# Attention and gated layer: stores of converted weights and of gated values, issued behind the next step

## The chip, the cores and the metric

The kernel runs on one core of a Trainium2 chip. The time is device microseconds (us) of one execution; the median of several runs counts. Five engines work side by side, each through its own queue and in order: PE (TensorE, matrix products), DVE (VectorE), ACT (ScalarE), POOL (GpSimd) and SP (SyncE, which issues most DMAs here). An instruction whose inputs are missing holds up all that stand behind it on its engine.

## The reference

Attention by random features over 8 batches, 8 heads, 576 positions of 64 values, then a gated layer over the 4608 tokens of 512 values:

```python
def phi(x):                                  # q and k, scaled before
    proj = np.einsum('bhsd,md->bhsm', x, omega)
    h = proj - np.sum(x * x, axis=-1, keepdims=True) / 2.0
    return np.exp(h - np.max(h, axis=-1, keepdims=True)) / np.sqrt(m)
...
kv = np.einsum('bhsm,bhsd->bhmd', k_p, v)
num = np.einsum('bhsm,bhmd->bhsd', q_p, kv)
...
x = np.ascontiguousarray(attn_out.transpose(0, 2, 1, 3)).reshape(B * S, H * D)
gate = 1.0 / (1.0 + np.exp(-(x @ w_gate)))
return (gate * (x @ w_val)) @ w_out          # 512 -> 1536 -> 512
```

The weights `w_gate`, `w_val` and `w_out` arrive as float64 and are converted on the chip.

## The kernel before

The program is written as Python generators. The order in which they record instructions is the program order; a scheduler then orders each engine's queue, by priorities and its own estimate of what is ready, and hands out tile buffers. An instruction passed through `pin` (`tc.keep_in_program_order`) may not stand ahead of the instruction that was recorded last before it on its engine; all others are free to move.

Stages, with their places in the profiled execution:

1. **Attention** (to about 510 us, `attention`, `norms`, `keys`, `queries`): for each of 4 batch pairs, two halves and 4 head pairs. A query step runs PE (projection `ppq`), DVE (`mxq`, `hmq`, `subq`, `hq`), PE (`ptq`), ACT (`qpq`), PE (`pnq`), DVE (`denq`, `invq`, `xq`), PE (`pxq`), ACT (`xsq`), and a DMA of ACT's queue to `xT` in DRAM. SP loads `rawk`, `rawq`, `natk`, `natq`, `v`.
2. **First pass** (`first_pass`, laced into the attention and running to about 590 us): columns 0 to 511 of the hidden layer for 10 chunks of tokens, named by their first token (0, 256, 512, 1024, ... 4096). A chunk's `xT` is loaded into `xr` (one buffer), ACT and POOL split it into four tiles `xe..._0` to `xe..._3` of a high and a low part, and for j = 0 to 3 PE makes two products `gv` of 12 matmuls, the gate (`gv..._j_0`, read by ACT into `ge`) and the value (`gv..._j_1`, read by DVE into `ye`, line 275). `ye` has two buffers and is stored to DRAM on SP (line 280). Until the attention is recorded to its end, the products have two PSUM banks.
3. **Conversion** (`convert_weights`): 14 tiles c0 to c13. Each is loaded on SP in two halves of 512 KB (line 144), each half takes six DVE operations (lines 78 to 94) and one of POOL (line 96), and the tile then four subtractions on POOL (`L180`); it is stored to `w32` in DRAM, 1 MB (line 181). There are two buffers `cv`. The generator `later` is advanced one step for each step of the first pass.
4. **Second pass** (from about 600 us, `second_pass`, `gated`), which needs `u0` to `u7`, loaded from `w32` and split (lines 199, 200, 214, 215); then the output product (`last`). The buffers of `u` and most of those that come late lie where the attention's buffers were, those of `cv` included, so `u0` is loaded only when they are free.

SP's queue is thus shared by the attention's loads, the first pass's loads and stores, and the conversion's loads and stores.

Of the kernel before, what the change touches and what calls it, by code (L numbers as in the profile page):

```python
# [34 lines left out]
NC = 512  # L35
Q = NC // 2
# [3 lines left out]
NE = 4  # L40
EP = NE // 2
WE = 2 * KC * P
# [25 lines left out]
def split(nc, hi, lo, x, lo_engine=None):  # L68

    nc.scalar.activation(out=hi, in_=x, func=AF.Copy)  # L70
    (lo_engine or nc.vector).tensor_tensor(out=lo, in0=x, in1=hi.bitcast(F32), op=ALU.subtract)  # L71


def from_float64(nc, t, a, bits):


    lo, hi = bits[:, :, 0], bits[:, :, 1]
    nc.vector.tensor_scalar(out=a, in0=hi, scalar1=0x7FFFFFFF, scalar2=None, op0=ALU.bitwise_and)

    f = a.bitcast(F32)  # L80
    nc.vector.tensor_scalar(
        out=f, in0=f, scalar1=LARGEST, scalar2=LEAST, op0=ALU.min, op1=ALU.max
    )

    nc.vector.tensor_scalar(
        out=t, in0=a, scalar1=3, scalar2=0x3FFFFFFF, op0=ALU.logical_shift_left, op1=ALU.bitwise_and
    )
    nc.vector.scalar_tensor_tensor(
        out=t, in0=hi, scalar=0xC0000000, in1=t, op0=ALU.bitwise_and, op1=ALU.bitwise_or
    )  # L90

    nc.vector.tensor_scalar(out=a, in0=t, scalar1=0xFF800000, scalar2=None, op0=ALU.bitwise_and)
    r = a.bitcast(F32)
    nc.vector.scalar_tensor_tensor(out=r, in0=lo, scalar=2.0**-52, in1=r, op0=ALU.mult, op1=ALU.mult)
    x = t.bitcast(F32)
    nc.gpsimd.tensor_tensor(out=x, in0=x, in1=r, op=ALU.add)
# [3 lines left out]
def attn_glu_kernel(ctx: ExitStack, tc, qT, kT, qn, kn, va, om, ident, w, out):  # L100
    nc = tc.nc
# [5 lines left out]
    w32 = dram.tile([N_LATE, P, 8, Q], F32, name="w32")  # L107


    ye = dram.tile([EP, P, NCH, 2, 2, 2, P], F32, name="ye")  # L110
# [16 lines left out]
    def any_bank(name):  # L127

        if not cycle:
            return bank("at", name)  # L130
        cycle.append(cycle.pop(0))
        return bank(cycle[-1], name)
# [3 lines left out]
    pin = tc.keep_in_program_order  # L136

    def converted(cv, i):


        raw = [cv[:, (1 + h) * 2 * WP : (2 + h) * 2 * WP] for h in range(2)]
        for h in range(2):
            o = i + h * WP
            nc.sync.dma_start(out=raw[h].rearrange("p (n two) -> p n two", two=2), in_=w[:, o : o + WP, :])
        yield
        for h in range(2):
            from_float64(
                nc, cv[:, h * WP : (h + 1) * WP], cv[:, 6 * WP :],
                raw[h].rearrange("p (n two) -> p n two", two=2),
            )  # L150
            yield
# [13 lines left out]

    def convert_weights(tiles, ns):

        for n in ns:
            cv = tiles(f"c{n}")
            for _ in converted(cv, NE * WE + n * 4 * Q):  # L170
                yield
            f = cv[:, : 4 * WP].bitcast(F32).rearrange("p (b q) -> p b q", q=Q)
            b, t = f[:, :4], f[:, 4:]
            for o, x, y in (
                (t[:, 0], b[:, 3], b[:, 0]),
                (t[:, 2], b[:, 2], b[:, 3]),
                (t[:, 1], b[:, 2], t[:, 0]),
                (t[:, 3], b[:, 1], t[:, 1]),
            ):
                nc.gpsimd.tensor_tensor(out=o, in0=x, in1=y, op=ALU.subtract)  # L180
            nc.sync.dma_start(out=w32[n], in_=f)


    turn = [0]
# [1 line left out]
    def buffer(name, dtype=F32R, at=None):  # L186
        if at is None:
            at = late if turn[0] % (XK + XL) < XL else keep
            turn[0] += 1
        return at.tile([P, 2, NC], dtype, tag="x", bufs=XK if at is keep else XL, name=name)  # L190
# [27 lines left out]
    def load(o, n):  # L218

        raw = keep.tile([P, KC, NC], F32, tag="xr", bufs=1, name=f"xr{o}_{turn[0]}")[:, :, :n]  # L220
        while not ready(o + n):
            next(steps, None)
        for k in range(KC):
            nc.sync.dma_start(out=raw[:, k], in_=xT[k, :, o : o + n])
        return raw

    def first_pass():


        def parts_of(o, n, at):  # L230
            raw = load(o, n)
            yield
            for k in range(KC):
                x = buffer(f"xe{o}_{k}", at=at)[:, :, :n]
                split(nc, x[:, 0], x[:, 1], raw[:, k], lo_engine=nc.gpsimd)
                yield x

        def product(i, j, o, n, x):
            name = f"gv{o}_{j}_{i}"
            gv = (any_bank(name) if late else bank("gv", name))[:, :n]  # L240
            wh, wl = ws[j]
            m = 0
            for k in range(KC):
                s = slice((i * KC + k) * P, (i * KC + k + 1) * P)
                xh, xl = x[k][:, 0], x[k][:, 1]
                for u, v in ((wl, xh), (wh, xl), (wh, xh)):
                    nc.tensor.matmul(gv, lhsT=u[:, s], rhs=v, start=(m == 0), stop=(m == 3 * KC - 1))  # L247
                    m += 1
            return gv


        chunks = [(0, Q), (Q, Q)] + [(c * NC, NC) for c in range(1, NCH)]
        x = [t for t in parts_of(*chunks[0], keep) if t is not None]
        at, homes = keep, []
        for (o, n), after in zip(chunks, chunks[1:] + [None]):
            ahead, parts = [], None
            for j in range(NE):
                if after and parts is None and (j == NE - 1 or late):

                    if late:  # L260
                        homes.append(keep if len(homes) % 2 == 0 else late)
                        at = homes[-1]
                    parts = parts_of(*after, at)
                    next(parts)
                gate = product(0, j, o, n, x)
                g = keep.tile([P, 2, 2, P], F32, tag="g", bufs=2, name=f"ge{o}_{j}")
                flat = g.rearrange("p i s t -> p (i s t)")[:, :n]
                nc.scalar.activation(out=flat, in_=gate, func=AF.Tanh, scale=0.5)
                yield
                if parts and at is late:  # L270
                    ahead += [t for t in (next(parts, None),) if t]
                val = product(1, j, o, n, x)
                y = keep.tile([P, 2, 2, P], F32, tag="y", bufs=2, name=f"ye{o}_{j}")

                nc.vector.scalar_tensor_tensor(
                    out=y.rearrange("p i s t -> p (i s t)")[:, :n], in0=flat, scalar=1.0, in1=val,
                    op0=ALU.add, op1=ALU.mult,
                )
                i = o % NC // Q
                nc.sync.dma_start(out=ye[j // 2, :, o // NC, j % 2, i : i + n // Q], in_=y[:, : n // Q])  # L280
                yield
            x = ahead + list(parts or ())

    def operands(c):

# [108 lines left out]
    def second_pass(x, parts):  # L394


        held = iter(())

        def put():
            while stores:  # L400
                to, y = stores.pop(0)
                pin(nc.sync.dma_start(out=to, in_=y))

        for c in range(NCH):
            ahead = None
            for pair in range(EP, NPAIR):
                g = keep.tile([P, 4, 2, P], F32, tag="g", bufs=2, name=f"gl{pair}_{c}")
                y = keep.tile([P, 2, N_OPS, P], F32, tag="y", bufs=2, name=f"yl{pair}_{c}")
                for kind in range(2):
                    group = gated(c, x, pair, kind, g, y)  # L410
                    next(group)
                    next(held, None)
                    next(group)
                    held = group
                    if pair == EP and kind:
                        assert next(parts, parts) is parts
                        if c < NCH - 1:
                            parts = operands(c + 1)
                            ahead = next(parts)
                    else:  # L420
                        next(parts, None)
                    yield c, pair, kind
                    if kind:
                        put()
            x = ahead
        next(held, None)
        yield NCH, EP, 0
        put()

    def gated_values(c, s, j, raw=None):  # L430
# [279 lines left out]
    stores = []  # L710
    with tc.tile_pool(name="early", bufs=1) as early:
        gates = first_pass()
        with tc.tile_pool(name="a", bufs=1, side="right") as pool:
            steps = attention(pool)

            def tiles(name):
                return pool.tile([P, 7 * WP], U32, tag="cv", bufs=2, name=name)
# [3 lines left out]
            n = 0  # L721
# [7 lines left out]
            n = credit = 0  # L729
# [136 lines left out]
```

## Time and profile before

| | |
|---|---|
| runs | 1236.67, 1238.58, 1239.37 us; median 1238.58 |
| the profiled execution | 1239.43 us, span 1237.6 us |
| mean granted clock of PE | 0.968 |
| chain that ended last | PE 71%, DVE 12%, issue 7%, DMA 5%, POOL 3% |
| DMA | 219.43 MB, 177 GB/s on average |

Times inside the execution are counted from the start of its span. The view of the busy time in stretches gives, for each engine, the busy us of that stretch, and behind them PE's granted clock, the busy share of the DMA engines and GB/s. In the view in order of time the first two numbers of a row are the start and the length, and a bracket at its end is the idle time before it with what ended it. `SPq` rows are DMA issues. A granted clock below 1.00 is the mean share of full speed that PE was given in the stretch.

### The profile page before, as it was taken

Reading aid. Unit: us, or ns where it says so; the run is one execution under the profiler, and the core shown is the slowest. Engines: PE = TensorE matmul, PEld = TensorE weight load, DVE = VectorE, ACT = ScalarE, POOL = GpSimd, SP = SyncE. Lnnn points to the kernel's source line nnn. Section 1 sums busy time; section 2 is a strip of 40 time slices with the busy share of each in tenths; the row PEclk is TensorE's granted clock in tenths of the full one; section 3 lists DMA queues with packets and bytes.
Section 4 is the critical chain, followed back from the end, with each engine's and each line's share of the span. In section 5 each row is a group of like instructions: output and inputs, shape, how many; then the busy total and the mean of one; then the engine's idle time right before and its main releaser. Section 6 shows DMA issues by size and latency. Waiting matters only on the chain.

```text
span 1237.6 us, 23990 instructions
## 1 busy us (share of the span) xinstructions
PE 1172.3 (95%) x8828; PEld 1109.8 (90%) x8828; DVE 864.5 (70%) x1907; ACT 530.7 (43%) x1164; POOL 542.7 (44%) x599
## 2 busy tenths in 40 slices
PE   6798989999898999899899999999998899999998
PEld 5788978798887888788899999999998899999998
DVE  4889888999698866433566656666569777777773
ACT  5556755565455463342423322232325344343331
POOL 2454365556457552131466666666666211111110
PEclk7798989999899999899899999999999999999999
DMA  7667767786657641461432333323337676666662
GB/s 247 213 199 228 210 219 253 238 268 237 226 182 252 223 153 39 139 202 52 152 128 106 123 135 124 121 93 125 124 135 267 203 226 195 188 191 189 198 191 94
DMA packets 104950, 219.43 MB, mean 177 GB/s; under 512 B 11136, under 2 KB 42112, under 8 KB 103040
## 3 DMA queue, kind: packets, MB, share of 16 engines
q1 hardware_dynamic: 87984, 198.94, 48.5%
q10 hardware_dynamic: 16848, 18.95, 4.4%
q8 instruction: 70, 1.15, 0.4%
q14 instruction: 48, 0.39, 0.1%
HBM read 141.82 MB, written 76.02 MB: 176 GB/s over the span
## 4 chain that ended last, share of the span: by engine, by line
PE 71%; DVE 12%; issue 7%; DMA 5%; POOL 3%; ACT 1%; SPq 1%; ACTq 0%; DVEq 0%; POOLq 0%
PE gw L351 27%; PE po L465 20%; PE gv L247 10%; PE pkv L595 4%; PE pnq L638 4%; PE ptq L626 2%; DVE mxq L552 2%; DVE hq L615 1%; DMA xr<-xT 1%; DMA xT<-xsq 1%; DMA rawk<-kT 1%; POOL loq L71 1%; DVE hmq L556 1%; PE ppk L547 1%; POOL xe L71 1%
## 5 line engine op out<-in xcount | busy, mean ns | idle before, releaser
L351 PE MATMUL gw<-xl,u 128*128 128x256 f32 x3024 | 364.6, 283 | 6.9 <-ACT p L362 3.6
L351 PEld LDWEIGHTS gw<-xl,u 128*128 128x128 f32 x3024 | 363.5, 191 | 7.9 <-DVE u L331 3.9
L465 PE MATMUL po<-u,yh 128*128 128x256 f32 x1512 | 272.4, 283 | 0.0
L465 PEld LDWEIGHTS po<-u,yh 128*128 128x128 f32 x1512 | 234.8, 191 | 0.0
L465 PE MATMUL po<-u,yl 128*128 128x256 f32 x756 | 214.0, 283 | 3.3 <-DVE yl L71 3.3
L247 PE MATMUL gv<-xe,wh 128*128 128x512 f32 (+1 forms) x640 | 201.0, 388 | 2.1 <-POOL xe L71 2.1
L70 ACT ACTIVATE yh<-yr 128x896 fp32r<-128x896 f32 x108 | 100.2, 950 | 156.8 <-PE po L465 86.3
L465 PEld LDWEIGHTS po<-u,yl 128*128 128x128 f32 x756 | 144.3, 191 | 3.9 <-DVE yl L71 3.9
L247 PEld LDWEIGHTS gv<-xe,wh 128*128 128x128 f32 x640 | 117.3, 194 | 20.1 <-POOL xe L71 4.5
L71 POOL TENSOR_TENSOR yl<-yr,yh 128x896 fp32r<-128x896 f32 x17 | 38.0, 2232 | 215.3 <-PE po L465 139.9
L247 PE MATMUL gv<-xe,wl 128*128 128x512 f32 (+1 forms) x320 | 125.8, 394 | 2.7 <-POOL wl L71 1.6
L71 DVE TENSOR_TENSOR yl<-yr,yh 128x896 fp32r<-128x896 f32 x91 | 103.0, 1144 | 31.5 <-PE po L465 19.1
L331 DVE TENSOR_TENSOR u<-gw,p 128x256 f32<-128x256 f32 x144 | 60.7, 422 | 59.2 <-PE gw L351 51.1
L595 PE MATMUL pkv<-v,kpk 128*128 128x66 f32 x512 | 84.4, 290 | 13.3 <-ACT kpk L587 12.6
L595 PEld LDWEIGHTS pkv<-v,kpk 128*128 128x128 f32 x512 | 77.0, 209 | 21.5 <-ACT kpk L587 19.8
L71 POOL TENSOR_TENSOR lok<-rawk,hik 128x256 fp32r<-128x256 f32 (+1 forms) x80 | 55.5, 712 | 68.0 <-ACT hik L70 67.6
L456 DVE TENSOR_TENSOR yr<-yr 128x128 f32<-128x128 f32 x144 | 60.1, 451 | 35.3 <-DMA yr<-ye 34.8
L71 POOL TENSOR_TENSOR xe<-xr,xe 128x512 fp32r<-128x512 f32 (+1 forms) x40 | 49.1, 1244 | 74.2 <-ACT xe L70 62.4
L71 POOL TENSOR_TENSOR loq<-rawq,hiq 128x256 fp32r<-128x256 f32 (+1 forms) x80 | 56.5, 718 | 55.5 <-ACT hiq L70 54.7
L587 ACT ACTIVATE kpk<-ppk,nb 128x128 f32<-128x128 f32 x256 | 69.8, 393 | 17.4 <-DVE nb L574 17.1
L638 PEld LDWEIGHTS pnq<-kv,qpq 128*128 128x128 f32 (+1 forms) x640 | 70.5, 189 | 6.5 <-ACT qpq L628 4.3
L638 PE MATMUL pnq<-kv,qpq 128*128 128x66 f32 (+1 forms) x640 | 74.9, 273 | 1.4 <-ACT qpq L628 1.2
(108 smaller groups left out, 2166.6 us busy)
## 6 DMA issues: line engine op xcount, KB each, us to landing
yl<-yl SPq DMA_DIRECT2D x36, 896.0 KB, 3.8
yr<-yl SPq DMA_DIRECT2D x72, 448.0 KB, 3.5
xr<-xT SPq DMA_DIRECT2D x68, 256.0 KB, 4.7
c<-w SPq DMA_DIRECT2D x28, 512.0 KB, 5.1
w<-c SPq DMA_DIRECT2D x14, 1024.0 KB, 4.5
v<-va SPq DMA_DIRECT2D x32, 330.0 KB, 3.4
natk<-kn SPq DMA_DIRECT2D x36, 256.0 KB, 4.2
natq<-qn SPq DMA_DIRECT2D x36, 256.0 KB, 3.9
```

The lines of the kernel that those rows point to most:

```text
L70: nc.scalar.activation(out=hi, in_=x, func=AF.Copy)
L71: (lo_engine or nc.vector).tensor_tensor(out=lo, in0=x, in1=hi.bitcast(F32), op=ALU.subtract)
L247: nc.tensor.matmul(gv, lhsT=u[:, s], rhs=v, start=(m == 0), stop=(m == 3 * KC - 1))
L331: return nc.vector.tensor_tensor(out=o, in0=a, in1=b, op=ALU.add)
L351: nc.tensor.matmul(o, lhsT=u[:, k, s], rhs=v[:, kc, :], start=(first and m == 0), stop=(m == 5), skip_group_check=not first,)
L456: nc.vector.tensor_tensor(out=raw[:, o], in0=raw[:, a], in1=raw[:, b], op=op)
L465: nc.tensor.matmul(o, lhsT=u[:, i, :], rhs=v[:, k, :], start=(j + m == 0 and n in (1, 6, 5, 4)), stop=(j == NPAIR - 1 and m == 2), skip_gr ...
L552: nc.vector.tensor_reduce(out=m.rearrange("p t h -> p (t h)"), in_=pp, axis=AX.X, op=ALU.max)
L587: nc.scalar.activation(out=kp[t][:, h, :], in_=pp[:, 2 * i + h, :], func=AF.Exp, bias=nb[:, t - t0, h : h + 1], scale=SCALE,)
L595: nc.tensor.matmul(pkv[:, h, :], lhsT=kp[b * MID + i][:, h, :], rhs=v[:, i, h, :], start=(i == 0), stop=(i == MID),)
L626: nc.tensor.transpose(out=pt[:, i, :], in_=h_sb[:, i, :], identity=id_sb)
L638: nc.tensor.matmul(pn[r, 2 * i + h, :], lhsT=qp[:, 2 * i + h, r], rhs=kvs[u, p, bb][:, h, :], start=True, stop=True,)
```

## The change

In `convert_weights` the store of tile n-1 is no longer issued when the tile is finished, but recorded behind the loads and the first converted half of tile n, and pinned there; the last one is pinned at the end. In `first_pass` the store of `ye` is put on a list, and `put` issues and pins what is on the list after the next gate's activation, and at the end of the pass. `put` itself is moved, unchanged, out of `second_pass`.

```diff
     def convert_weights(tiles, ns):
 
+        made = None
         for n in ns:
             cv = tiles(f"c{n}")
-            for _ in converted(cv, NE * WE + n * 4 * Q):
+            for i, _ in enumerate(converted(cv, NE * WE + n * 4 * Q)):
+                if i == 1 and made:
+                    pin(nc.sync.dma_start(out=w32[n - 1], in_=made))
                 yield
...
-            nc.sync.dma_start(out=w32[n], in_=f)
+            made = f
+        pin(nc.sync.dma_start(out=w32[n], in_=made))
...
+    def put():
+        while stores:
+            to, y = stores.pop(0)
+            pin(nc.sync.dma_start(out=to, in_=y))
+
     def first_pass():
...
                 nc.scalar.activation(out=flat, in_=gate, func=AF.Tanh, scale=0.5)
+                put()
                 yield
...
-                nc.sync.dma_start(out=ye[j // 2, :, o // NC, j % 2, i : i + n // Q], in_=y[:, : n // Q])
+                stores.append((ye[j // 2, :, o // NC, j % 2, i : i + n // Q], y[:, : n // Q]))
                 yield
             x = ahead + list(parts or ())
+        put()
```

What the scheduler makes of it: up to tile c2 the engines' queues stay nearly the same. Then each store that is tied behind some load stands where that load stands, and the buffers `cv` come free later: the store of c1 now stands behind that of c2, that of c6 behind that of c7, and c3, c5, c7, c8 and c9 are loaded where the program before loads about c4, c7, c9, c11 and c12. The largest difference is at the end of the attention. SP there, before (numbers behind a name's last underscore are the buffer's), from the store of c12 to the first load of `u0`:

```order
L181 DMA w32_64<-c12_7180 128x2048
L280 DMA ye_65<-ye2048_2_6065 128x512
L519 DMA rawq3_2_1_6550<-qT 128x640
L519 DMA rawq3_3_1_6604<-qT 128x640
L571 DMA v3_3_1_6497<-va 128x660
L181 DMA w32_64<-c13_7202 128x2048
L280 DMA ye_65<-ye2048_3_6402 128x512
L224 DMA xr3072_0_7244<-xT_63 128x512 x4
L280 DMA ye_65<-ye2560_0_6643 128x512
L280 DMA ye_65<-ye2560_1_6920 128x512
L199 DMA u0_7280<-w32_64 128x768
```

And now SP from the store of `ye2560_0` to the same load (c10 has been loaded ahead of the load of `xr3072`, at the place of `v3_3_1`):

```order
L234 DMA ye_65<-ye2560_0_6643 128x512
L173 DMA w32_64<-c9_6385 128x2048
L144 DMA c11_7157<-w 128x1024 x2
L173 DMA w32_64<-c10_6747 128x2048
L234 DMA ye_65<-ye2560_1_6920 128x512
L144 DMA c12_7179<-w 128x1024 x2
L173 DMA w32_64<-c11_7157 128x2048
L144 DMA c13_7201<-w 128x1024 x2
L173 DMA w32_64<-c12_7179 128x2048
L234 DMA ye_65<-ye2560_2_7241 128x512
L185 DMA w32_64<-c13_7201 128x2048
L228 DMA xr3584_0_7306<-xT_63 128x512 x3
```

Before, all of the conversion stood ahead of the load of `xr3072`; now the stores of c9 to c13 and the loads of c11 to c13 stand behind it, and each load waits for the store two tiles earlier. DVE at the end of the attention's last head pair, now (before, the rows of c12 and c13 are not there, and `ye2560_2` follows `xq3_3_7` directly):

```order
L621 SCALAR_TENSOR_TENSOR hq3_3_7_7098<-ppq3_3_7_7086,subq3_3_7_7096 128x512
L653 RECIPROCAL invq3_1_7_7107<-denq3_1_7_7105 128x4
L81 TENSOR_SCALAR c12_7179<-c12_7179 128x512
L655 TENSOR_TENSOR xq3_1_7_7109<-pnq3_1_7_7100,invq3_1_7_7107 128x256
L85 TENSOR_SCALAR c12_7179<-c12_7179 128x512
L88 SCALAR_TENSOR_TENSOR c12_7179<-c12_7179 128x512
L649 TENSOR_SCALAR denq3_3_7_7141<-pnq3_3_7_7136 128x4
L92 TENSOR_SCALAR c12_7179<-c12_7179 128x512
L653 RECIPROCAL invq3_3_7_7143<-denq3_3_7_7141 128x4
L94 SCALAR_TENSOR_TENSOR c12_7179<-c12_7179 128x512
L655 TENSOR_TENSOR xq3_3_7_7145<-pnq3_3_7_7136,invq3_3_7_7143 128x256
L78 TENSOR_SCALAR c13_7201<-c13_7201 128x512
```

Behind these rows come the other eleven operations of c13, six ahead of `ye2560_2` and six ahead of `ye2560_3` in all, so the conversion now shares DVE with the attention's last steps. POOL at the split of chunk 3072 (`xe3072`), now:

```order
L71 TENSOR_TENSOR loq3_3_7_7030<-rawq3_3_1_6604,hiq3_3_7_7029 128x256
L96 TENSOR_TENSOR c11_7157<-c11_7157 128x512 x2
L183 TENSOR_TENSOR c11_7157<-c11_7157 128x256 x4
L96 TENSOR_TENSOR c12_7179<-c12_7179 128x512 x2
L183 TENSOR_TENSOR c12_7179<-c12_7179 128x256 x4
L96 TENSOR_TENSOR c13_7201<-c13_7201 128x512 x2
L71 TENSOR_TENSOR xe3072_1_7297<-xr3072_0_7243,xe3072_1_7297 128x512
L183 TENSOR_TENSOR c13_7201<-c13_7201 128x256 x3
L71 TENSOR_TENSOR xe3072_2_7300<-xr3072_0_7243,xe3072_2_7300 128x512
L183 TENSOR_TENSOR c13_7201<-c13_7201 128x256
L71 TENSOR_TENSOR xe3072_3_7303<-xr3072_0_7243,xe3072_3_7303 128x512
```

Before, `xe3072_1` follows `loq3_3_7` directly and the three `xe3072` rows stand together; now eighteen operations of c11 to c13 stand ahead of or among them.

More of the change, by code (lines that the diff above doesn't have):

```diff
@@ L397, in second_pass @@
         held = iter(())
[L399 to L402, printed above, removed]
         for c in range(NCH):
```

## The prediction

> **What bounds the kernel now.** I read the page first, then the busy time in stretches of 50 us over the part in which the change moves something, then SP's waits.
>
> ```profile
> PE 1172.3 (95%) x8828; PEld 1109.8 (90%) x8828; DVE 864.5 (70%) x1907; ACT 530.7 (43%) x1164; POOL 542.7 (44%) x599
> ```
> ```profile
> 200.00:250.00 50.00, 46.31 (x321) 38.16 (x320) 45.17 (x104) 26.82 (x75) 27.24 (x32) 1.00 0.68 223
> 250.00:300.00 50.00, 49.24 (x353) 43.89 (x352) 45.51 (x117) 33.65 (x95) 27.25 (x34) 1.00 0.80 274
> 300.00:350.00 50.00, 46.60 (x307) 42.72 (x306) 36.96 (x98) 25.56 (x74) 27.93 (x33) 0.90 0.59 206
> 350.00:400.00 50.00, 45.52 (x331) 38.98 (x331) 45.00 (x111) 24.38 (x66) 30.37 (x35) 1.00 0.66 222
> 400.00:450.00 50.00, 48.28 (x355) 43.87 (x355) 42.17 (x115) 25.04 (x70) 27.62 (x33) 1.00 0.54 179
> 450.00:500.00 50.00, 47.65 (x344) 41.05 (x343) 30.38 (x83) 23.82 (x68) 14.44 (x19) 1.00 0.26 91
> ```
> PE is busy 95% of the span, so a gain can only come out of PE's idle time and out of stretches at a low clock. From 200 to 450 us PE is idle 3.7 + 0.8 + 3.4 + 4.5 + 1.7 = 14.1 us, and the clock of 0.90 in one row costs (1 - 0.90) x 50 = 5.0 us more: **19 us is the most that can be won there**. DVE is nearly as full as PE: 214.8 of 250 us. Behind 450 us DVE drops to 30.4 of 50 and the DMA engines to a share of 0.26. So the conversion sits in the fullest part, and there is room behind it.
>
> ```profile
> SPq L280 <- DVE ye L275: 73.0, 18, 16.3
> SPq L181 <- POOL c L180: 60.8, 11, 12.1
> ```
> SP stood 60.8 us, in 11 places, with the store of a converted tile at its head, and 73.0 us with a store of `ye`. What stands behind such a store is held up. One place shows what that can cost:
>
> ```profile
> 296.64 0.53 SPq L499 DMA_DIRECT2D natq<-qn  x1
> 305.90 0.33 SPq L181 DMA_DIRECT2D w<-c  x1
> 306.32 1.35 SPq L499 DMA_DIRECT2D natq<-qn  x2
> ```
> ```profile
> 310.00:320.00 10.00, 7.62 (x52) 6.41 (x50) 8.82 (x26) 4.52 (x12) 4.50 (x6) 1.00 1.02 365
> 320.00:330.00 10.00, 9.18 (x46) 9.00 (x47) 2.17 (x10) 3.66 (x12) 1.26 (x1) 0.59 0.36 120
> ```
> SP is blocked from 297.2 to 305.9 by the store of c6; then everything goes out at once (DMA share 1.02), PE idles 2.4 + 0.8 us, and then runs at 0.59, which costs 4.1 us more: **7.3 us in one place**.
>
> **The change part by part.** It adds and removes no work. It moves 14 stores of 1 MB and the stores of `ye`, and with them, through the two buffers `cv`, the conversion of the later tiles. The cost of one tile:
>
> ```profile
> L180 POOL TENSOR_TENSOR c<-c x56: 722/740/1193, 154.3 to 450.5; 128x256 f32<-128x256 f32 x56
> L78 DVE TENSOR_SCALAR c<-c x28: 409/424/1496, 102.4 to 434.1; 128x512 uint32<-128x512 uint32 x28
> L81 DVE TENSOR_SCALAR c<-c x28: 397/416/1372, 114.1 to 439.5; 128x512 f32<-128x512 f32 x28
> L85 DVE TENSOR_SCALAR c<-c x28: 394/418/922, 114.8 to 440.5; 128x512 uint32<-128x512 uint32 x28
> L88 DVE SCALAR_TENSOR_TENSOR c<-c x28: 661/682/1527, 122.3 to 442.6; 128x512 uint32<-128x512 uint32 x28
> L92 DVE TENSOR_SCALAR c<-c x28: 396/416/1044, 129.6 to 444.1; 128x512 uint32<-128x512 uint32 x28
> L94 DVE SCALAR_TENSOR_TENSOR c<-c x28: 660/682/1350, 131.9 to 446.2; 128x512 f32<-128x512 uint32 x28
> L96 POOL TENSOR_TENSOR c<-c x28: 1269/1285/1662, 133.1 to 447.0; 128x512 f32<-128x512 f32 x28
> ```
> ```profile
> c<-w SPq DMA_DIRECT2D x28, 512.0 KB, 5.1
> w<-c SPq DMA_DIRECT2D x14, 1024.0 KB, 4.5
> ```
> By the medians a half costs DVE 0.42 + 0.42 + 0.42 + 0.68 + 0.42 + 0.68 = 3.04 us, a tile 6.1; POOL 2 x 1.29 + 4 x 0.74 = 5.5. A load lands after 5.1, a store after 4.5.
>
> *From 200 to 450 us.* By the orders, four tiles (c10 to c13) leave this part. That takes 4 x 6.1 = 24.4 us off DVE (11% of its 214.8), 22 us off POOL and 8 MB off the DMA queues. At the place of the 7.3 us two stores (c3, c4) now find finished tiles and the `natq` loads stand behind the `xr` loads, but the loads of c5 and c6 (2 MB) stand ahead of these. The bounds are 0 and 7.3; I take the half, 3.7. Of the other idle time, 14.1 - 3.2 = 10.9 us, the bounds are 0 and all; a quarter seems fair for 11% less load on an engine that is 86% full: 2.7. Against that, DVE meets two tiles earlier than they land: c4's loads stand among those of chunk 1536 and c7's behind the store of c5, and its first operation stands at most one load time (5.1 us) ahead of the landing, at least none. I take 2 us each, and that PE, which has other products to run, loses half: 2. **Gain 3.7 + 2.7 - 2 = 4.4 us**, between -5 and +18.
>
> *The end of the attention.* Here the change adds a chain that runs through SP, DVE and POOL:
>
> ```profile
> 473.16 17.01 SPq L280 DMA_DIRECT2D ye<-ye  x2
> 510.74 0.32 SPq L199 DMA_DIRECT2D u<-w  x1
> ```
> ```profile
> 497.97 0.69 DVE L615 SCALAR_TENSOR_TENSOR hq<-ppq,subq 128x512 f32<-128x512 f32 x1
> 506.78 0.16 DVE L643 TENSOR_SCALAR denq<-pnq 128x4 f32<-128x4 f32 x1 [2.46 <-PE pnq L638]
> 513.47 0.69 DVE L275 SCALAR_TENSOR_TENSOR ye<-ge,gv 128x512 f32<-128x512 f32 x1 [5.85 <-PE gv L247]
> 518.89 0.69 DVE L275 SCALAR_TENSOR_TENSOR ye<-ge,gv 128x512 f32<-128x512 f32 x1 [0.40 <-PE gv L247]
> ```
> ```profile
> 481.55 0.74 POOL L71 TENSOR_TENSOR loq<-rawq,hiq 128x256 fp32r<-128x256 f32 x1 [0.30 <-ACT hiq L70]
> 518.10 4.03 POOL L71 TENSOR_TENSOR xe<-xr,xe 128x512 fp32r<-128x512 f32 x3 [35.82 <-ACT xe L70]
> ```
> In the times of before: `ye2560_0` is stored at 473.2, c9 right behind; it lands 4.5 later, at 478, and c11 another 5.1 later, at 483. c12 is loaded behind the store of `ye2560_1`, which came at 490 (the end of the first row) and comes somewhat earlier now, since its last product stands ahead of three transposes in PE's new order; so it lands by 495. DVE works on c11 and c12 between the attention's last operations. Ahead of the last `hq` of that group (497.97) stand three operations of c11 and one of c12, 0.68 + 0.42 + 0.68 + 0.42 = 2.2 us, and one more (0.42) ahead of the `hq` of the last head pair; the other five of c12's half mostly fall into DVE's idle 2.46 us. So the attention ends **2.7 us later**. The bounds are nothing, if DVE's gaps hold all, and the whole 2 x 6.1 = 12.2.
>
> c11 is through DVE at about 500 and through POOL 1.3 + 3.0 later, at 504; its store lands at 508.5, and c13 at 513.6. Its two halves on DVE then end at about 516.7 and, with `ye2560_2` between, at 520, and POOL's second `L96` at 521. POOL was idle for 35.82 us ahead of `xe3072_1`; now it is not: `xe3072_1` could start at 518.1 + 2.7 = 520.8 and starts at 521, and four subtractions of c13 (4 x 0.74 = 3.0) stand among the three splits. PE waits for the last of them: **3.1 us**, with bounds 0 and c13's whole 5.5.
>
> The clock. PE then idles about 5 us in 7. Two rows show what followed such idling before, the one above (2.4 us idle, then 0.59) and this one:
>
> ```profile
> 500.00:510.00 10.00, 7.79 (x50) 6.58 (x50) 4.22 (x16) 2.09 (x6) 0.00 (x0) 0.81 0.15 50
> 510.00:520.00 10.00, 9.39 (x35) 7.30 (x34) 2.34 (x3) 3.08 (x6) 1.90 (x2) 0.85 0.62 183
> ```
> There 2.2 us idle went with (0.19 + 0.15) x 10 = **3.4 us** lost to the clock. I add that once; the bounds are 0 and 2 x 3.4.
>
> The Trainium skill, in "TensorE: Matmul & The Clock Gate", Part 1, says that the clock falls to half after at least one idle window of about 3.4 us. By that rule single waits of 1 to 3 us would leave the clock alone, and my sum would lose its 3.4 us. The rows above speak against so strict a reading: 2.4 us of idle time in 10 were followed by 0.59.
>
> *What is hidden.* The loads of `u0` to `u4` waited for the attention's end (510.74); now they also wait until the store of c13 has landed, at about 526.9 + 4.5 = 531.4. ACT and DVE take them in order, between `ge3072`, `xe3584_3` and `ye3072_1`.
>
> ```profile
> 514.55 0.43 SPq L200 DMA_DIRECT2D u<-w  x1
> 532.04 1.06 ACT L214 ACTIVATE u<-u 128x1024 fp32r<-128x1024 f32 x1 [0.41 <-DMA u<-w]
> ```
> Before, they took from 514.55 to 532.0, so now to about 549. PE has products that don't need them: one product takes 2.7 us (half of 518.89 - 513.47, for a pair), and from about 528, when the splits of chunk 3072 are done, seven and a half such products run to 548 or 549. The cover holds, with nothing to spare. I cost it at nothing, and 4 us if it is gone. Later stores of `ye` wait little, and the second pass, whose SP order is the same, begins later by what is lost.
>
> **The sum**: 2.7 + 3.1 + 3.4 = 9.2 lost, 4.4 won: 1239.4 + 4.8 = 1244.2 for the profiled execution, which lies 0.85 above the median of the runs: **1243.4 us**.
>
> **The rivals.**
> - *The middle wins* (faster). Stores that no longer stand unfinished at SP's head, with four tiles less, give back 12 of the 19 us, and the end costs the 5.8 without a new clock loss: 1238.6 - 6.2 = 1232.4. For it speaks the place at 297 us, against it that many of PE's idle times end with DVE's or ACT's own chain. It decides the sign from the point where the middle gives over 5.8 + 2.5 = 8.3, or over 11.7 if the clock is lost at the end. Chance 0.28.
> - *It cancels*: the middle gives 9 (half of 19), the end costs 9.2: 1238.8. Or the stores' new places are not felt, because SP's waits were covered anyway: 1238.6. Together 0.12.
> - *The clock stays up* at the end, by the mechanism of waits too short: 1243.4 - 3.4 = 1240.0, which is within 0.2%. Chance 0.10.
> - *The cover is gone*: `u4` lands late, ACT holds `ge3072_3` and `xe3584_3`, PE waits 4 us and the clock falls again: 1243.4 + 4 + 3.4 = 1250.8. Chance 0.12.
>
> **How the numbers follow.** My forecast has 0.38, with a range of its own of 1241 to 1247. 0.2% (2.5 us) is about what a measurement of this kernel can tell from no change. Slower: 0.38 + 0.12 = 0.50; same: 0.12 + 0.10 = 0.22; faster: 0.28. The range reaches from 1232, the first rival, to 1253, the last with 2 us more for the bounds of the first term.
>
> **What would show it.** Right: the last `xq` of DVE 2 to 4 us later against `ye2560_0`; c's operations on DVE and POOL until past 515 us; POOL's three `xe3072` over 7 us instead of 4.03; a second stretch of low clock behind them; `u0` loaded some 20 us later. Wrong: if PE's idle time from 200 to 450 falls below 5 us, or if c13 lands before 505 us, or if PE waits at chunk 3584.

## The result and the profile after

The changed kernel takes 1247.91 us (median of 16 runs, 1239.35 to 1256.52) against 1236.6 us of the kernel before on the same chip (16 runs, 1229.87 to 1242.54). The ratio is 1.0092, with a 95% interval of 1.0063 to 1.0121: **slower by 0.9%, some 11.4 us** (0.0092 x 1237). The forecast was 1243.4 us, slower by 4.8.

The profiled execution of the changed kernel took 1256.42 us, span 1254.6, granted clock 0.956. It lies 8.5 us above its own median, so the sums taken from it are larger than the 11.4 us to be explained; a second profile of the same kernel (e12, below) has a span of 1247.3. The first value `ye0_0` comes 2.1 us later than in the profile of before (79.31 against 77.22), ahead of anything that was moved. That is chance: in the profiles of all kernels here it comes between 74.0 and 79.6 us, and in e12 at 74.1.

The busy time of the changed kernel in stretches of 50 us (columns as in the rows of before: PE, PEld, DVE, ACT, POOL, clock, DMA share, GB/s):

```profile
200.00:250.00 50.00, 47.78 (x348) 41.92 (x348) 37.74 (x108) 30.09 (x85) 22.34 (x28) 1.00 0.61 199
250.00:300.00 50.00, 47.84 (x344) 42.67 (x343) 41.78 (x104) 33.25 (x94) 22.22 (x30) 1.00 0.79 261
300.00:350.00 50.00, 46.16 (x311) 42.53 (x309) 37.30 (x95) 25.68 (x73) 24.83 (x29) 0.91 0.66 222
350.00:400.00 50.00, 46.88 (x309) 41.00 (x309) 34.23 (x95) 23.19 (x64) 23.04 (x28) 0.88 0.53 172
400.00:450.00 50.00, 47.20 (x337) 42.38 (x335) 39.64 (x99) 23.96 (x67) 22.60 (x28) 1.00 0.35 113
450.00:500.00 50.00, 46.86 (x336) 41.28 (x335) 34.11 (x93) 22.48 (x67) 19.93 (x24) 0.97 0.57 192
500.00:550.00 50.00, 41.01 (x181) 33.26 (x181) 29.34 (x66) 12.75 (x23) 24.23 (x23) 0.80 0.46 162
```

From 200 to 450 us DVE's work fell from 214.8 to 190.7 us, and PE's idle time stayed at 250 - 235.9 = 14.1 us. The row that stands out is the last: 9.0 us idle and a clock of 0.80. The stretch around the attention's end in one row, before and then after:

```profile
490.00:550.00 60.00, 56.56 (x275) 45.70 (x274) 26.61 (x51) 24.62 (x41) 14.67 (x11) 0.94 0.49 160
```
```profile
490.00:550.00 60.00, 50.81 (x250) 42.15 (x251) 37.52 (x92) 16.04 (x29) 25.52 (x24) 0.83 0.51 182
```

Idle time is 60 - 56.56 = 3.4 us before and 9.2 after; the clock takes (1 - 0.94) x 60 = 3.6 us before and 10.2 after. DVE does 10.9 us more work in that stretch and POOL 10.9 more. SP there, in order of time in the changed kernel:

```profile
512.41 0.33 SPq L173 DMA_DIRECT2D w<-c  x1
516.75 0.80 SPq L144 DMA_DIRECT2D c<-w  x2
525.06 0.33 SPq L173 DMA_DIRECT2D w<-c  x1
526.84 0.33 SPq L234 DMA_DIRECT2D ye<-ye  x1
537.29 0.32 SPq L185 DMA_DIRECT2D w<-c  x1
538.52 2.10 SPq L228 DMA_DIRECT2D xr<-xT  x3
541.64 0.32 SPq L203 DMA_DIRECT2D u<-w  x1
```

These are the store of c11, the loads of c13, the stores of c12, of `ye2560_2` and of c13, three loads of `xr3584`, and the first load of `u0`, which stood at 510.74 before. What it does on DVE, in order of time:

```profile
507.16 0.69 DVE L621 SCALAR_TENSOR_TENSOR hq<-ppq,subq 128x512 f32<-128x512 f32 x1
507.76 0.89 DVE L85 TENSOR_SCALAR c<-c 128x512 uint32<-128x512 uint32 x1
508.69 1.10 DVE L88 SCALAR_TENSOR_TENSOR c<-c 128x512 uint32<-128x512 uint32 x1
509.82 0.84 DVE L92 TENSOR_SCALAR c<-c 128x512 uint32<-128x512 uint32 x1
510.58 0.15 DVE L649 TENSOR_SCALAR denq<-pnq 128x4 f32<-128x4 f32 x1
510.69 1.10 DVE L94 SCALAR_TENSOR_TENSOR c<-c 128x512 f32<-128x512 uint32 x1
511.71 0.16 DVE L653 RECIPROCAL invq<-denq 128x4 f32<-128x4 f32 x1
...
519.85 0.42 DVE L655 TENSOR_TENSOR xq<-pnq,invq 128x256 f32<-128x256 f32 x1
```

Between the attention's `hq` and its `denq` and `invq` stand four operations of c12, and they take 0.89 + 1.10 + 0.84 + 1.10 = 3.9 us where the medians of before give 0.42 + 0.68 + 0.42 + 0.68 = 2.2. POOL's rows show what ran beside them, and what follows at chunk 3072:

```profile
508.45 3.93 POOL L183 TENSOR_TENSOR c<-c 128x256 f32<-128x256 f32 x4
...
530.80 1.29 POOL L96 TENSOR_TENSOR c<-c 128x512 f32<-128x512 f32 x1 [3.38 <-DVE c L94]
532.04 1.26 POOL L71 TENSOR_TENSOR xe<-xr,xe 128x512 fp32r<-128x512 f32 x1
533.26 2.10 POOL L183 TENSOR_TENSOR c<-c 128x256 f32<-128x256 f32 x3
535.32 1.26 POOL L71 TENSOR_TENSOR xe<-xr,xe 128x512 fp32r<-128x512 f32 x1
536.54 0.72 POOL L183 TENSOR_TENSOR c<-c 128x256 f32<-128x256 f32 x1
537.22 1.27 POOL L71 TENSOR_TENSOR xe<-xr,xe 128x512 fp32r<-128x512 f32 x1
```

c11's four subtractions ran beside the last three of the four operations of c12 (beside the first, POOL was finishing an addition, `L96`), and were slower themselves (3.93 us for four, 0.98 each, against 0.74). Further down, c13's last addition and its subtractions stand ahead of and among the three splits of chunk 3072, which end at 538.49. What PE waited for, first in the changed kernel from 500 to 550 us, then in the kernel before from 490 to 540 (us in total, times, longest):

```profile
PE gv L256 <- POOL xe L71: 4.2, 3, 2.3
PE pxq L661 <- DVE xq L655: 1.7, 1, 1.7
PE ptq L632 <- DVE hq L621: 1.1, 1, 1.1
PE ptq L632 <- DVE hmq L562: 1.0, 1, 1.0
```
```profile
PE gv L247 <- POOL xe L71: 1.2, 3, 0.6
PE pxq L655 <- DVE xq L649: 1.0, 1, 1.0
```

Behind it PE waits for nothing up to 610 us. The busy time from 540 to 610 us in the changed kernel:

```profile
540.00:610.00 70.00, 70.00 (x326) 58.35 (x325) 25.91 (x34) 26.88 (x41) 14.63 (x11) 0.98 0.52 179
```

PE does not wait at chunk 3584, nor for the late `u0`, though `u4` was through DVE only at 560.8 (its row starts at 559.54).

### The profile page after: what moved, and what is told of

Its sections match the earlier page's. It is cut to its first block, busy times and chain, and to the rows that moved or that the text cites. A ratio compares the mean times of both kernels' runs of the same rounds, so it can differ in the third digit from the quotient of the medians.

```text
span 1254.6 us, 23989 instructions
## 1 busy us (share of the span) xinstructions
PE 1182.6 (94%) x8828; PEld 1122.3 (89%) x8828; DVE 863.7 (69%) x1907; ACT 530.7 (42%) x1164; POOL 538.0 (43%) x599
## 4 chain that ended last, share of the span: by engine, by line
PE 73%; DVE 10%; DMA 5%; issue 5%; POOL 4%; ACT 2%; SPq 1%; ACTq 0%; DVEq 0%; POOLq 0%
PE gw L362 26%; PE po L471 20%; PE gv L256 11%; PE pnq L644 4%; PE pkv L601 4%; PE ptq L632 2%; DVE mxq L558 1%; DMA c<-w 1%; DMA xT<-xsq 1%; DVE hq L621 1%; DMA xr<-xT 1%; POOL xe L71 1%; PE ppk L553 1%; POOL c L96 1%; PE ppk L555 1%
## 5 line engine op out<-in xcount | busy, mean ns | idle before, releaser
L256 PEld LDWEIGHTS gv<-xe,wh 128*128 128x128 f32 x640 | 119.0, 197 | 24.1 <-POOL xe L71 7.8
L71 DVE TENSOR_TENSOR yl<-yr,yh 128x896 fp32r<-128x896 f32 x91 | 100.6, 1123 | 26.0 <-PE po L471 13.1
L601 PE MATMUL pkv<-v,kpk 128*128 128x66 f32 x512 | 87.7, 301 | 15.5 <-ACT kpk L593 15.2
L601 PEld LDWEIGHTS pkv<-v,kpk 128*128 128x128 f32 x512 | 80.9, 221 | 22.5 <-ACT kpk L593 20.8
L462 DVE TENSOR_TENSOR yr<-yr 128x128 f32<-128x128 f32 x144 | 64.1, 479 | 42.8 <-DMA yr<-ye 42.3
L644 PEld LDWEIGHTS pnq<-kv,qpq 128*128 128x128 f32 (+1 forms) x640 | 73.6, 196 | 5.3 <-ACT qpq L634 3.4
```

The source lines that it names most:

```text
L462: nc.vector.tensor_tensor(out=raw[:, o], in0=raw[:, a], in1=raw[:, b], op=op)
L601: nc.tensor.matmul(pkv[:, h, :], lhsT=kp[b * MID + i][:, h, :], rhs=v[:, i, h, :], start=(i == 0), stop=(i == MID),)
L644: nc.tensor.matmul(pn[r, 2 * i + h, :], lhsT=qp[:, 2 * i + h, r], rhs=kvs[u, p, bb][:, h, :], start=True, stop=True,)
```

## The experiments

My theory after these traces: the stores' ties push c11 to c13 into the attention's end, and all of the loss arises there, by three ways (DVE's share, POOL's share, the clock). The rivals: the stores of `ye` are at fault, or the middle. By its own order, which was not run, the scheduler puts the later-recorded stores of the tiles back where they were when the ties are left out, so it is the tie, not the place in the program, that moves them.

**e1: only the stores of `ye` moved and tied.** The loop of `convert_weights` is that of before:

```diff
-                if i == 1 and made:
-                    pin(nc.sync.dma_start(out=w32[n - 1], in_=made))
...
-            made = f
-        pin(nc.sync.dma_start(out=w32[n], in_=made))
+            nc.sync.dma_start(out=w32[n], in_=f)
```

> Only the stores of ye are moved and tied, the converted tiles are stored as before; the instruction order of PE, ACT and POOL is that of before, and c13 is stored ahead of xr3072 as before. Theory (the tied stores of the converted tiles carry the loss, by pushing c10 to c13 into the attention's end): within 2 us of before. Rival (the tied ye stores carry it, since SP stood 80.8 us with one of them at its head): 8 to 12 us slower than before. Third (the ye stores are a gain that the tiles' stores hide): 2 to 5 us faster.

Measured 0.9996 of before (0.9971 to 1.0021). The `ye` stores cost and win nothing that can be measured, though SP still stood 67.8 us with one at its head in this kernel (80.8 in the changed one, 73.0 before).

**e2: only the stores of the tiles moved and tied.**

```diff
-                stores.append((ye[j // 2, :, o // NC, j % 2, i : i + n // Q], y[:, : n // Q]))
+                nc.sync.dma_start(out=ye[j // 2, :, o // NC, j % 2, i : i + n // Q], in_=y[:, : n // Q])
```

> Only the stores of the converted tiles are moved and tied, ye is stored as before. c11 and c12 are loaded one store of ye earlier than in the changed kernel, c13 still behind ye2560_1, u0 behind ye2560_3 in place of behind xr3584. Theory: 8 to 12 us slower than before, with low clock and three xe3072 over 6 us at the attention's end. Rival (ye stores): within 2 us of before.

Measured 1.0102 (1.0063 to 1.0141), 12.6 us, just above the theory's range: all of the loss. From 490 to 550 us its PE was idle for 6.6 us at a clock of 0.83.

**e3: ties for c0 to c6 only.**

```diff
-                    pin(nc.sync.dma_start(out=w32[n - 1], in_=made))
+                    (pin if n - 1 < 7 else lambda v: v)(nc.sync.dma_start(out=w32[n - 1], in_=made))
...
-        pin(nc.sync.dma_start(out=w32[n], in_=made))
+        nc.sync.dma_start(out=w32[n], in_=made)
```

> The change with the ties of the tiles' stores kept for c0 to c6 and left off from c7 on: the middle is ordered as in the changed kernel up to the load of c9, behind that the conversion catches up (c13 is loaded ahead of ye2560_0 and stored ahead of the first u0, which stands where it did before). Theory: the middle alone costs 0 to 4 us, so 0 to 4 us slower than before, and the attention's end looks like before (xe3072 three times in 4 to 5 us, no half clock behind 510 us but one). Rival (the middle carries the loss, as 5.5 of the 17 us of the two profiled executions would have it, or all of it): 6 to 11 us slower.

Measured 1.0015 (0.9989 to 1.0041): the reordered middle costs 1.9 us or nothing, not 6 to 11. The busy time shows where the caught-up tiles went:

```profile
450.00:490.00 40.00, 34.17 (x221) 29.79 (x222) 29.97 (x75) 17.20 (x54) 23.61 (x29) 0.87 0.45 164
490.00:510.00 20.00, 19.83 (x148) 17.66 (x147) 14.86 (x47) 6.29 (x12) 4.31 (x6) 1.00 0.25 94
510.00:530.00 20.00, 16.61 (x78) 12.53 (x77) 7.29 (x16) 8.74 (x15) 4.02 (x3) 1.00 0.59 195
```

In this one execution PE was idle for 5.8 us from 450 to 490 us and the clock took 5.2 (2.3 and 0 before), and the end gave some of it back. Whether the three tiles cost anything there is not shown: the interval reaches from 1.4 us faster to 5.1 slower. They cost less than at the attention's end.

**e4: ties from c9 on only** (the same edit with `n - 1 >= 9`).

> The change with the ties left off for c0 to c8 and kept for c9 to c13: the tiles are loaded and stored as before up to the load of c10, and from the store of c9 (behind ye2560_0) on as in the changed kernel. Theory: the attention's end carries the loss, 8 to 12 us slower than before, with DVE working on c11 to c13 between 490 and 530 us and PE's clock below 0.9 there. Rival (the middle carries it): within 2 us of before, since PE has other work at the end.

Measured 1.0084 (1.0056 to 1.0113), 10.4 of the 11.4 us, with the middle as before. e3 and e4 together: **the loss lies at the attention's end.**

**e5: POOL's subtractions of c11 to c13 out.**

```diff
-                nc.gpsimd.tensor_tensor(out=o, in0=x, in1=y, op=ALU.subtract)
+                if n < 11:
+                    nc.gpsimd.tensor_tensor(out=o, in0=x, in1=y, op=ALU.subtract)
...
+            for half in (slice(0, 4), slice(4, 8)):
+                pin(nc.sync.dma_start(out=w32[n, :, half], in_=f[:, :4]))
```

> The changed kernel without POOL's four subtractions of c11, c12 and c13; each of these tiles is stored as its first half twice, so w32 holds no differences for the last three tiles. All other instructions stand in the changed kernel's order. In the changed kernel's profile DVE's operations of c12 and c13 took 0.84 to 1.10 us wherever POOL's subtractions ran beside them, in place of 0.42 and 0.68, and POOL's splits xe3072 stood between c13's subtractions. Theory (a part of the loss at the attention's end comes by way of POOL: slower DVE beside it, and the splits behind the subtractions): 4 to 7 us slower than before in place of 11, three xe3072 within 4.5 us, and DVE's operations of c12 at 0.42 and 0.68. Rival (DVE's share alone carries it): 9 to 12 us slower. Second rival (the late loads of u0 carry it, which are not touched): 9 to 12 us slower.

Measured 1.0035 (1.0011 to 1.0059): 4.3 us in place of 11.4, and the two intervals (1.4 to 7.3 and 7.8 to 15.0 us) lie apart, so a good part of the loss, some 7 us by the middle values, goes with POOL's subtractions. Its DVE rows in order of time, at the place shown above, and its POOL rows:

```profile
499.86 0.43 DVE L92 TENSOR_SCALAR c<-c 128x512 uint32<-128x512 uint32 x1
500.20 0.15 DVE L657 TENSOR_SCALAR denq<-pnq 128x4 f32<-128x4 f32 x1
500.32 0.69 DVE L94 SCALAR_TENSOR_TENSOR c<-c 128x512 f32<-128x512 uint32 x1
```
```profile
518.19 3.76 POOL L71 TENSOR_TENSOR xe<-xr,xe 128x512 fp32r<-128x512 f32 x3
```

These operations are back at 0.43 and 0.69, and the three splits take 3.76 us in one piece in place of 6.45. (The first of the four, `L85` at 498.21, still takes 0.89: it runs beside POOL's addition `L96`, which this edit leaves in.) The edit does a third thing, which the expectation left out: the chain itself is shorter without the subtractions. The last store of c13 is issued 48.4 us behind the start of `ye2560_0` on DVE in place of 57.5, and `u0` 53.2 in place of 61.9. So e5 does not divide the 7 us between slower operations on DVE, later splits and a shorter chain.

**e6: c13 out.**

```diff
-        for n in ns:
+        for n in ns[:-1]:
...
+        pin(nc.sync.dma_start(out=w32[n + 1], in_=made))
```

> The changed kernel without the conversion of c13 (its loads, twelve operations of DVE and six of POOL are left out); c12's tile is stored a second time in its place. Theory (c11 and c12 cost the attention's last head pair some 4.6 us, c13 the splits of chunk 3072 some 5.7 us): 5 to 7 us slower than before. Rival (c11 and c12 with the clock carry all): 9 to 12 us slower. Second rival (it is the sheer lateness of the last tile and of u0 behind it): 0 to 3 us slower.

Measured 1.0061 (1.0035 to 1.0087), 7.5 us: half a microsecond above what the theory gave, and not near 0 to 3. The second rival isn't settled by that, for `u0` is still late in this kernel: it is loaded 54.8 us behind `ye2560_0`, against 38.3 before and 61.9 in the changed kernel. What speaks against it is the row from 540 to 610 us above, in which PE waits for nothing. The interval overlaps that of the changed kernel, so c13's share (some 4 us by the middle values) isn't well measured.

**e7: the splits of chunk 3072 on DVE.**

```diff
-                split(nc, x[:, 0], x[:, 1], raw[:, k], lo_engine=nc.gpsimd)
+                split(nc, x[:, 0], x[:, 1], raw[:, k], lo_engine=nc.vector if o in (3072,) else nc.gpsimd)
```

> The changed kernel with the splits xe3072 on DVE in place of POOL, all four. They then stand behind c13's last operations on DVE and ahead of ye2560_3, and no longer between c13's subtractions. Theory (the splits' place behind POOL's subtractions costs 3 to 6 us, DVE finishes c13 at 530.7 in the profile of the changed kernel and can split at 0.7 us each): 7 to 10 us slower than before. Rival (PE waits there for the gate and for DVE anyway): 10 to 13 us slower.

Measured 1.0065 (1.004 to 1.0089), 8.0 us: in the theory's range, 3.4 us below the changed kernel, but the two intervals overlap. Inconclusive as to size.

**e8: the kernel before with the tiles stored by POOL.**

```diff
-            nc.sync.dma_start(out=w32[n], in_=f)
+            nc.gpsimd.dma_start(out=w32[n], in_=f)
```

> The kernel before with the stores of the converted tiles issued by POOL behind its own last subtraction, so that none stands unfinished at SP's head. Theory of the prediction's first term (SP's 60.8 us with such a store at its head cost PE up to 7.3 us at 297 to 330 us and some beside): 3 to 8 us faster than before. Rival (other waits take its place, PE's idle time in the middle ends with DVE's and ACT's chains): within 2 us. Second rival (POOL's issue of a 1 MB store costs POOL time): 2 to 6 us slower.

Measured 1.0208 (1.0173 to 1.0243), 25.7 us slower: a miss of all three. SP's waits from 200 to 500 us in this kernel:

```profile
SPq L519 <- POOL lok L71: 41.0, 14, 10.4
SPq L571 <- PE pkv L595: 28.9, 11, 10.2
SPq L519 <- POOL loq L71: 25.7, 15, 7.3
SPq L571 <- PE pxq L655: 22.5, 3, 12.8
SPq L144 <- DMA w<-c: 21.8, 8, 5.7
```

No finished tile stands at SP's head any more, and SP waits for free buffers instead: 66.7 us for those of `raw` (37.3 before, `L519`, by the same view), and 21.8 us with the load of the next tile for the store to land. So taking that wait away won nothing here, and other waits took its place. The loss lies in the middle: from 200 to 450 us PE was idle for 23.6 us and the clock took 17.5, against 14.0 and 5.0 before. The order of all engines changed with this edit, and what brings these 22 us stays open.

**e9: c12 and c13 out.**

```diff
-        for n in ns:
+        for n in ns[:-2]:
...
-        pin(nc.sync.dma_start(out=w32[n], in_=made))
+        for k in range(n, n + 3):
+            pin(nc.sync.dma_start(out=w32[k], in_=made))
```

> The changed kernel without the conversion of c12 and c13 (loads, DVE's and POOL's operations left out); c11's tile is stored three times. The middle up to the load of c11 is that of the changed kernel. Theory (what is left of the loss in e5 and e6 is c12's share of DVE among the attention's last operations; the middle gives nothing): 0 to 3 us slower than before. Rival (the middle, reordered by the ties, costs some 4 us by itself): 4 to 7 us slower.

Measured 1.0000 (0.9971 to 1.003). The middle is that of the changed kernel up to the load of c11, and without the last two tiles nothing is lost and nothing is won, within some 3.6 us. The row of its end:

```profile
490.00:550.00 60.00, 56.68 (x254) 45.69 (x254) 21.90 (x35) 21.98 (x35) 17.95 (x16) 0.94 0.65 229
```

That is 3.3 us idle and 3.6 of clock, as before the change.

**e10: the changed kernel with the conversion started earlier**, and **e11: the kernel before with the same edit.**

```diff
-FROM = 20
+FROM = 14
```

> The changed kernel with the conversion of c0 started six steps of the first pass earlier (FROM 14 in place of 20). All ties are kept, but c13 is loaded at ye2560_0 in place of ye2560_1 and converted ahead of the last head pair's last steps, and its store and the first u0 stand at ye2560_1, as in the kernel before. Theory (the ties cost nothing by themselves, only the lateness of the last tiles): 0 to 4 us slower than before. Rival (the ties cost wherever the tiles end): 8 to 12 us slower. Second rival (earlier stores in the middle are the gain that the change was short of): 2 to 6 us faster.

> The kernel before with the conversion of c0 started six steps earlier, no ties. Theory: c13 is stored at the same place as before, so the attention's end stays as it is, and the middle is as full as before: within 3 us of before. Rival (the conversion's early tiles crowd the start, where PE is least busy): 3 to 8 us slower. Second rival (work is drawn out of the fullest part): 3 to 8 us faster.

e10 measured 0.9988 (0.9964 to 1.0012), e11 1.0073 (1.0045 to 1.0102). With the ties kept and the tiles early, the 11.4 us are gone (1.5 us faster by the middle value, just outside the theory's 0 to 4 slower): it is not the ties as such that cost. The same earlier start makes the kernel before 9.0 us slower, which my expectation missed. In its profile PE is idle for 6.8 us from 200 to 250 us, at a clock of 0.90, where before it was 3.7 at 1.00; what causes that was not tried. e10 and e11 differ by the change alone, and their intervals lie apart: with the early start the change is worth some 10 us, where with the late one it costs 11.4. Its sign hangs on when the conversion starts. e10 is level with the kernel before, and none of these versions beats it by more than a measurement can tell.

**e12: the changed kernel again**, unedited, for a second profile.

> The changed kernel a second time, for its profile. Theory: PE's idle time and clock loss between the last transposes of the second half's fourth head pair and the value of ye3584_1 repeat within 3 us (some 9 us idle and a clock of 0.85 to 0.92), as do DVE's long operations of c12 and c13 beside POOL; the half clocks in the middle (348, 392 and 461 us) need not come again. Rival (the end's loss of the first profile was chance): idle time below 6 us and a clock above 0.94 there.

```profile
490.00:550.00 60.00, 50.89 (x227) 41.67 (x226) 36.73 (x75) 18.46 (x30) 25.51 (x24) 0.80 0.52 187
```

The end repeats: 9.1 us idle and 12.0 of clock. The expectation erred on the middle: half clocks came there again, near 315, 345 and 390 us.

All profiles beside the measured times, each in us: idle time of PE plus (1 - clock) x the stretch, from the rows of the busy time, and last the time from the start of `ye2560_0` on DVE to that of `ye3584_1` (before: 472.44 to 552.60). That last column needs no sum, and it begins and ends at the same work in every kernel:

| kernel | against before | 200 to 450 | 490 to 550 | `ye2560_0` to `ye3584_1` |
|---|---|---|---|---|
| before | 0 | 14.0 + 5.0 | 3.4 + 3.6 | 80.2 |
| e1, `ye` only | -0.5 | 14.0 + 5.0 | 4.4 + 1.8 | 79.7 |
| e9, without c12, c13 | 0.0 | 14.8 + 0 | 3.3 + 3.6 | 80.7 |
| e3, ties to c6 | 1.9 | 15.4 + 7.5 | 3.6 + 0 | 78.0 |
| e5, without POOL's part | 4.3 | 13.5 + 2.5 | 7.3 + 1.8 | 83.2 |
| e6, without c13 | 7.5 | 13.4 + 5.0 | 6.6 + 6.6 | 86.9 |
| e7, splits on DVE | 8.0 | 12.4 + 7.5 | 9.6 + 3.6 | 91.6 |
| e4, ties from c9 | 10.4 | 12.3 + 5.0 | 8.5 + 13.8 | 93.4 |
| the change, two profiles | 11.4 | 14.1 + 10.0, 14.8 + 10.0 | 9.2 + 10.2, 9.1 + 12.0 | 91.1, 91.8 |
| e2, tiles only | 12.6 | 13.1 + 7.5 | 6.6 + 10.2 | 92.9 |
| e10, the change, early start | -1.5 | 15.1 + 2.5 | 4.9 + 3.6 | 81.6 |
| e11, before, early start | 9.0 | 18.5 + 10.0 | 4.9 + 1.8 | 80.0 |
| e8, stores on POOL | 25.7 | 23.6 + 17.5 | 4.7 + 1.8 | 79.1 |

Each row is one execution, which can lie well off the median (e5's 4.9 us and e9's 5.2 below, the first of the change 8.5 above), and a clock of two digits over 250 us makes steps of 2.5 us. Among the kernels with ties, down to e10, the middle's idle time does not follow the times; the last column does, to within some 4 us, and grows by 10.9 and 11.6 us with the change. In e11 and e8, which have no ties, PE loses more in the middle instead. One thing stays open: in both profiles of the change the way from `ye1536_0` to `ye2560_0` is also longer, 147.6 and 147.5 us against 139.9, while the times of e3 and e9 show little or no loss from that middle.

## Why the prediction came out as it did

The sign, the place and the range were right. The range took in both signs, so that it held says little; the forecast's own 1241 to 1247 was missed by 0.9 us. The size came out at 11.4 us where the sum gave 4.8, and the difference lies mainly in two terms, a gain that did not come and a loss that was larger.

- **The middle, a gain of 4.4: this step failed.** Its cause happened in full: DVE lost 214.81 - 190.70 = 24.1 us of work (24.4 forecast), POOL 25.4 (22 forecast). Its effect didn't. PE's idle time was 14.0 before and 14.1 and 14.8 in two profiles after, and the clock took more, not less. At 300 to 340 us the changed kernel did better in its first profile (2.0 us idle and 3.4 of clock, against 3.4 and 5.2, so 3.2 won where 3.7 were forecast), but in its second by 0.8 only, and new half clocks near 345 and 390 us took it back. e9 and e3 put the middle as a whole at 0.0 and 1.9 us lost. The step from a fuller DVE to PE's idle time, "a quarter seems fair", had no row behind it. PE's longest waits from 200 to 500 us in the kernel before (total, times, longest):

```profile
PE pkv L595 <- ACT kpk L587: 6.5, 7, 2.5
PE pxq L655 <- DVE xq L649: 3.6, 4, 1.8
```

  6.5 of the 16.4 us that PE was idle there end with ACT's `kpk`. But these rows would not have settled it: with the shorter ones, 7.9 us end with DVE and 7.9 with ACT, and `kpk` itself stood 10.0 us behind DVE's `nb`. In the two profiles after, 5.5 and 8.2 us end with DVE, 11.3 and 9.9 with ACT. So the runs show that 24 us less work on DVE did not shorten PE's waits, and that its waits for ACT grew; why, stays open. For SP's part, e8 shows that other waits can take the place of those with a store.
- **The attention's end, 2.7 us later: right in PE's idle time, too small on DVE.** Idle time rose by 9.2 - 3.4 = 5.8 us in the stretch, as 2.7 + 3.1 said (and by 5.7 in the second profile). The last `xq` came 519.85 - 479.79 = 40.1 us behind `ye2560_0`, against 507.19 - 472.44 = 34.8: 5.3 us later, not the 2 to 4 that I named. Part of that may be the clock (0.67 from 510 to 520 us), part is the 1.7 us by which c12's four operations ran longer beside POOL, which the medians I used didn't hold.
- **POOL's splits, 3.1 us: right.** PE waited 4.2 us for them where it waited 1.2. The three took 6.45 us, not "over 7". They start at 532.04, not 521, but two thirds of that lie ahead of the place: SP stored `ye2560_0` at 480.50 in this profile, 7.3 us later than before. Counted from that store, c11 was through POOL after 31.9 us (30.8 forecast) and c13 was there for DVE after 40.3 (40.4 forecast), so the chain through SP, DVE and POOL ran as worked out; then c13's first half took 0.74 + 0.84 + 0.83 + 1.10 + 0.84 + 0.69 = 5.0 us, most of it beside c12's subtractions, in place of 3.04, and the first split came after 51.5 us (47.8 forecast). `u0` was loaded 31 us later than before, 23.6 counted from the store, where 20 were forecast.
- **The clock, 3.4 us: mis-sized.** It took 10.2 - 3.6 = 6.6 us more in the first profile and 8.4 in the second, about the upper bound that I gave (twice 3.4) or above it. The clock listed with every run says the same for the whole kernel: (1 - clock) x span is 45.7 us on average over the 16 runs of the changed kernel and 35.0 over the 27 runs of the kernel before that were taken with e1 to e4. These 10.7 us are nearly the whole loss by themselves. Since (1 - clock) x time also counts what PE was idle at a low clock, idle time and clock can't be added up exactly, and how the 11.4 us divide between them stays open.
- **The cover, at nothing: right, with less to spare than thought.** PE is full from 540 to 610 us.
- **The rivals.** The first and the second (the middle gives 12, or 9) are refuted by e9 and e3, the third (the clock stays up) by the rows. That the cover goes did not happen, though its time, 1250.8, lies nearer to the result than my forecast: a near time with a cause that was absent.

With the middle at 0 and the clock at 6.6, the sum is 2.7 + 3.1 + 6.6 = 12.4, inside the measured 7.8 to 15.0; that is a sum after the fact, with the two terms taken from the result.

## What to carry to other kernels

A tie on a store is a tie on the buffer that it frees: with two buffers, each load waits for the store two tiles earlier, so follow the last tile of the chain and ask what it now runs beside. Work taken off an engine that is nearly full need not buy anything: 24 us less on DVE left PE's idle time where it was, although half of PE's waits had ended with DVE. A share of the idle time that merely seems fair is no estimate. Before a schedule's edit is dropped, move the whole chain, with the edit and without it (here an earlier start, e10 and e11): the edit and its lateness are two things.

## What the runs showed of the hardware

**DVE and POOL slow each other.** DVE's operations of 128x512 took 0.83 to 1.10 us beside POOL's subtractions of 128x256 in place of 0.42 and 0.68, and the subtractions 0.98 in place of 0.74; with the subtractions out (e5) those of DVE that had run beside them were back at 0.43 and 0.69, and only beside POOL's addition `L96` did two others still take longer (0.89 and 1.38). The Trainium skill says in "SBUF — State Buffer", section "Who interferes with whom", that a DVE instruction with two inputs in SBUF contends with a GpSimd instruction that reads SBUF. The rows agree for the two operations of a half that have two inputs (lines 88 and 94, from 0.68 to 1.10); those with one input (lines 81, 85 and 92) went from 0.42 to 0.83 and 0.84, and that sentence does not speak of them.

**The clock falls without a long wait.** In the changed kernel PE's longest single wait from 500 to 550 us was 2.3 us (the row of `xe` above), and up to 530 us it was 1.7. Yet the clock was at 0.67 to 0.80 in three stretches in a row:

```profile
500.00:510.00 10.00, 7.90 (x55) 6.90 (x54) 9.78 (x26) 3.04 (x6) 3.00 (x3) 0.93 0.09 28
510.00:520.00 10.00, 7.77 (x41) 6.87 (x40) 7.76 (x24) 1.71 (x4) 3.53 (x4) 0.67 0.54 194
520.00:530.00 10.00, 9.58 (x33) 7.78 (x34) 8.41 (x13) 1.51 (x3) 6.16 (x6) 0.72 0.51 201
530.00:540.00 10.00, 5.77 (x18) 3.57 (x17) 1.38 (x2) 1.57 (x4) 7.69 (x8) 0.80 0.19 79
```

The rule of the Trainium skill that the prediction weighed ("TensorE: Matmul & The Clock Gate", Part 1: half the clock after an idle window of about 3.4 us) doesn't hold here if the window is read as a single wait; several short ones, 2.1 and 2.2 us in 10, went with the fall. How much idle time it takes no run here shows: from 490 to 550 us, 9.6 us of it went with 3.6 us lost to the clock in e7, and 8.5 us with 13.8 in e4.
